# Sliding-window attention and a GELU layer on one core: key loads on a second queue, chunked V copies, other engines for three evictions

## The chip, the core and the metric

The kernel runs on one core of a Trainium2 chip. The core has TensorE (matrix products, into the accumulator memory PSUM), VectorE, ScalarE and GpSimd (elementwise work), SyncE (which issues transfers here) and 16 DMA engines. In the profile they are PE (and PEld for its weight loads), DVE, ACT, POOL and SP. The metric is the device time of one execution in microseconds.[...]

## What is computed

Attention over 8 batches of 8 heads, 576 positions and 64 features, in which a position sees only those up to 32 away; its result, as 4608 tokens of 512 features, goes through a layer with 2048 hidden features and a tanh-GELU.

```python
scores = scale * np.matmul(q, k.transpose(0, 1, 3, 2))
mask = np.abs(pos[:, None] - pos[None, :]) <= window          # window = 32
scores = np.where(mask, scores, -1000000000.0)
attn = softmax(scores)                                        # cut: row maximum, exp, sum
attn_out = np.matmul(attn, v)
x = attn_out.transpose(0, 2, 1, 3).reshape(B * S, H * D)      # 4608 x 512
h = x @ w_in                                                  # 512 x 2048
g = 0.5 * h * (1.0 + np.tanh(c * (h + 0.044715 * h * h * h)))
out = g @ w_out                                               # 2048 x 512
```

## The kernel before

The tokens are split into 9 tiles of 512. Tile t goes through `ffn_in` (512-wide products with w_in, then GELU on ScalarE) and `ffn_out` (products with w_out). Beside the `ffn_out` of tile t the attention of batch t+1 is computed, piece by piece: a plan says ahead of which matmul of `ffn_out` (its place, `i`) which piece is put into the program. In the plans, s is the scores of a pair of heads, m their mask, v their sums and values with the inversion of the sums on ScalarE, x the product that writes them to the tokens, and d the copy of one chunk of V. The number after the letter is the pair of heads (−1: the last positions of the batch before), the number after @ a PSUM buffer.

```python
PLAN = {4: "s0@0 s1@1 v-1", 16: "m0 m1 x-1", 33: "s2@0 v0@1 v1", 36: "m2", ...}     # tiles 2 to 6
PLAN_1 = {12: "s0@0 s1@1 s2", 16: "m0 m1", 36: "m2", 45: "v0@1 v1 s-1@0", 52: "x0", 55: "x1", 62: "m-1",
          69: "s3@0 v2 v-1@1", 73: "m3", 81: "x2", 85: "x-1", 91: "v3 s4@1", 112: "x3 m4"}   # tile 1
PAIR_1 = {17: slice(0, 4), 40: slice(4, 8)}
```

Queries and keys are loaded as fp32, cast to fp16 on VectorE and transposed by DMA. For batch 2 the loads are put into the program near the end of tile 0, and the V loads stand behind the key transposes on SyncE.

```python
def load_qk(b):
    ...
    nc.sync.dma_start(qr, q[b, :, 0:512, :].rearrange("h (p j) d -> p h (j d)", j=4))
    for c in range(4):
        nc.sync.dma_start(kr[:, c, :, :],
                          k[b, :, 128 * c:128 * c + 128, :].rearrange("h p d -> p h d"))
    nc.sync.dma_start(qt, ...)          # the last 64 positions
    nc.sync.dma_start(kt, ...)

def keys():                             # in tile 1, behind the casts of the queries, two combines and sums
    for pr in range(NPAIR):
        nc.vector.tensor_copy(k16[:, pr, :, :, :], kr[:, :, 2 * pr:2 * pr + 2, :])
        if pr % 2:
            nc.sync.dma_start_transpose(KTs[b % 2][...], k16[...])
    if b == 2:
        for c in range(4):
            nc.sync.dma_start(vr[:, c, :, :], v[b, ...])
```

The values need V twice: as loaded, and with the two halves of its 128 partitions shifted against each other (slots 4 to 7). For batch 2 GpSimd casts the four chunks, and `pair_v` copies the shifted half on VectorE, four heads at a time; `pair_chunk`, which tile 0 uses, copies one chunk of all heads.

```python
def pair_v(b, copy, hs=slice(0, H)):
    copy(V[64:128, 4:8, hs, :], V[64:128, 0:4, hs, :])
    copy(V[0:64, 4:7, hs, :], V[0:64, 1:4, hs, :])

def pair_chunk(b, c, copy):
    copy(V[64:128, 4 + c, :, :], V[64:128, c, :, :])
    if c:
        copy(V[0:64, 3 + c, :, :], V[0:64, c, :, :])
...
            if t == 1 and i in PAIR_1:
                pair_v(2, nc.vector.tensor_copy, PAIR_1[i])
```

Tile 0 has four accumulators of 128 tokens, finished in the order 0, 3, 1, 2. Accumulator 0 is in the bank that the first `ffn_in` of tile 1 takes. The other tiles use a product scheme with fewer matmuls (seven products of 16 matmuls each, n = 0 to 6), whose two banks take turns: product 0 and then 2 in one, product 1 and then 3 in the other, and product 4 takes the first one again. So the bank has to be read between product 0 and 2 (`M1`), and between 2 and 4 (`C11`).

```python
# ffn_out_0, tile 0
(nc.scalar.copy if t4 > 1 else nc.vector.tensor_copy)(yo, pys[t4])
# ffn_out, tiles 1 to 8
if n == 0:
    nc.vector.tensor_copy(M1, py)                                    # L653
elif n == 1:
    nc.vector.tensor_tensor(U2, py, M1, op=ALU.add)                  # L655
elif n == 2:
    (nc.vector.tensor_copy if t > 1 else nc.scalar.copy)(C11, py)    # L657
```

Of the kernel before, what the change touches and what calls it, by code (L numbers as in the profile page):

```python
# [36 lines left out]
def cut(b):  # L37
# [5 lines left out]

PLAN = {4: "s0@0 s1@1 v-1", 16: "m0 m1 x-1", 33: "s2@0 v0@1 v1", 36: "m2", 44: "x0", 50: "x1",
        62: "s3@0 s4@1 v2", 66: "m3", 80: "x2", 84: "m4", 91: "v3", 112: "x3"}


# [4 lines left out]
          29: "w2", 33: "s-1@1 n0@0", 35: "e0", 36: "m2", 37: "k3", 38: "w5", 39: "m-1", 40: "r3@1", 43: "e1",  # L54
          46: "s3@0 v-1@1 d0", 47: "w3 e2", 48: "d1 m3", 51: "n2@0", 52: "e3 d2 d3 x-1",
          55: "u3 p0@0 p2@1 x0 x1", 56: "e4 x2 x3", 60: "c1"}
PLAN_1 = {12: "s0@0 s1@1 s2", 16: "m0 m1", 36: "m2", 45: "v0@1 v1 s-1@0", 52: "x0", 55: "x1", 62: "m-1",
          69: "s3@0 v2 v-1@1", 73: "m3", 81: "x2", 85: "x-1", 91: "v3 s4@1", 112: "x3 m4"}
PAIR_1 = {17: slice(0, 4), 40: slice(4, 8)}

ORDER_0 = [(t4, 4 * w + i) for w in range(3) for i in ((0, 2, 3, 1), (0, 2, 1, 3), range(4))[w] for t4 in (0, 1, 3, 2)] + \
          [(t4, 12 + i + j) for i in (0, 2) for t4 in (0, 3, 1, 2) for j in range(2)]
# [7 lines left out]
def kernel(  # L70
# [9 lines left out]
    nc = tc.nc  # L80
# [82 lines left out]
    def load_qk(b):  # L163


        qr = rawp.tile([128, H, 256], FP32, name="qr")
        kr = rawp.tile([128, 4, H, 64], FP32, name="kr")
        qt = tailp.tile([16, H, 256], FP32, name="qt", tag="vt")
        kt = tailp.tile([64, H, 64], FP32, name="kt", tag="tr")
        raws[b] = (qr, kr, qt, kt)  # L170
        nc.sync.dma_start(qr, q[b, :, 0:512, :].rearrange("h (p j) d -> p h (j d)", j=4))
        for c in range(4):
            nc.sync.dma_start(kr[:, c, :, :],  # L173
                              k[b, :, 128 * c:128 * c + 128, :].rearrange("h p d -> p h d"))
        nc.sync.dma_start(qt, q[b, :, 512:576, :].rearrange("h (p j) d -> p h (j d)", j=4))  # L175
        nc.sync.dma_start(kt, k[b, :, 512:576, :].rearrange("h p d -> p h d"))

# [9 lines left out]
    def pair_v(b, copy, hs=slice(0, H)):  # L187

        V = Vs[b % 2]
        copy(V[64:128, 4:8, hs, :], V[64:128, 0:4, hs, :])  # L190
        copy(V[0:64, 4:7, hs, :], V[0:64, 1:4, hs, :])  # L191
# [143 lines left out]
    def bank(i):  # L335

        return psM.tile([128, 512], FP32, name="mm", tag=f"x{i}")
# [140 lines left out]
    def weigh(b, g, pair=None):  # L478
        pe = groups.pop((b, g))
        if pair is not None:  # L480
            od = psS.tile([128, 2, 512], FP32, name="ps_od", tag=f"S{pair}")
            o, d = od[:, 0, :], od[:, 1, :]
        else:
            o = psO.tile([128, 512], FP32, name="ps_o", tag="O")
            d = psO.tile([128, 512], FP32, name="ps_d", tag="D")
        sum_up(b, g, d, pe)
        times(b, g, o, pe)
        return o, d
# [101 lines left out]
    pys = {}  # L590

    def store(t, t4, yo, cols=slice(0, 512), *engs):

        m = i = 0
        while m < 128:
            b, c = divmod(t * 512 + t4 * 128 + m, S)
            q0, n = (0, cut(b)) if c < 4 * cut(b) else (cut(b), 144 - cut(b))
            j, p = divmod(c - 4 * q0, n)
            e = min(n - p, 128 - m)
            nj = 1 if p else max(1, min(4 - j, (128 - m) // n))  # L600
            eng = engs[i % len(engs)] if engs else nc.gpsimd
            if nj > 1:
                e = nj * n
                eng.dma_start(out_v[b, j:j + nj, q0:q0 + n, cols], yo[m:m + e, cols])
            else:
                eng.dma_start(out_v[b, j, q0 + p:q0 + p + e, cols], yo[m:m + e, cols])  # L606
            m += e
            i += 1
# [3 lines left out]
    def ffn_out_0(t4, fc):  # L612
        new = t4 not in pys
        if new:
            pys[t4] = bank(t4) if t4 < 2 else psO.tile([128, 512], FP32, name="py3", tag="OD"[t4 % 2])
        nc.tensor.matmul(pys[t4], gTs[0][:, fc, t4 * 128:t4 * 128 + 128], w_out16[:, fc, :],
                         start=new, stop=(fc == NF - 1))
        if fc == NF - 1:
            if "yo" not in pys:
                pys["yo"] = hp.tile([128, 2, 512], FP32, name="yo2", tag="qt16")  # L620
            yo = pys["yo"][:, t4, :] if t4 < 2 else yp.tile([128, 512], FP32, name="yo", tag="yo")
            (nc.scalar.copy if t4 > 1 else nc.vector.tensor_copy)(yo, pys[t4])  # L622
            later.append((t4, yo))

    def ffn_out(t, i):

        n, blk, f = i // 16, i // 8 % 2, i % 8
        a, w, new = WINO[n]
        end = t == NT - 1
        if i % 16 == 0 and new:  # L630
            pys[n % 2] = bank((1 + n) % 2)
            if end and n == 4:
                pys["apart"] = psO.tile([128, 512], FP32, name="py2", tag="O")
        py = pys[n % 2].rearrange("p (b c) -> p b c", b=2)
        apart = end and blk and n in (4, 6)
        if a[0] == "A":
            r0, c0 = 8 * (int(a[2]) - 1) + f, 256 * (int(a[1]) - 1) + 128 * blk
            lhsT = gTs[t][:, r0, c0:c0 + 128]
        else:
            lhsT = wino[a][:, f, 128 * blk:128 * blk + 128]  # L640
        one = end and n in (4, 6)
        nc.tensor.matmul(pys["apart"][:, 0:256] if apart else py[:, blk, :], lhsT,  # L642
                         wino[w][:, f, :], start=(new and i % (8 if one else 16) == 0),
                         stop=(i % (8 if one else 16) == (7 if one else 15)),
                         skip_group_check=True)
        if i % 16 < 15:
            return
        yo, left, right = wino["yo"], slice(0, 256), slice(256, 512)
        C11, C12, C21, C22 = (yo[:, r:r + 2, c] for r in (0, 2) for c in (left, right))

        M1, U2, U3 = C21, C12, C22
        if n == 0:
            nc.vector.tensor_copy(M1, py)  # L653
        elif n == 1:
            nc.vector.tensor_tensor(U2, py, M1, op=ALU.add)  # L655
        elif n == 2:
            (nc.vector.tensor_copy if t > 1 else nc.scalar.copy)(C11, py)  # L657
            if end:
                for x in range(2):
                    store(t, x, yo[:, x, :], left, nc.sync)  # L660
        elif n == 3:
            nc.vector.tensor_tensor(U3, py, M1, op=ALU.add)
        elif n == 4:
            if not end:
                nc.vector.tensor_tensor(C22, py, U3, op=ALU.add)
            else:
                for x, part in enumerate((py[:, 0, :], pys["apart"][:, 0:256])):
                    nc.vector.tensor_tensor(C22[:, x, :], part, U3[:, x, :], op=ALU.add)
                    store(t, 2 + x, yo[:, 2 + x, :], right, nc.sync, nc.scalar)
        elif n == 5:  # L670
            nc.vector.tensor_tensor(C21, py, M1, op=ALU.add)  # L671
            for x in range(2):
                store(t, 2 + x, yo[:, 2 + x, :], *((left, nc.sync, nc.scalar) if end else ()))
# [78 lines left out]
    s0 = psS.tile([128, 2, 512], FP32, name="ps_o", tag="S0")  # L752
# [63 lines left out]
    for t in range(NT):  # L816
        b = t + 1
        att = b < B
        if t:
# [6 lines left out]
            for fc in range(begun, NF):  # L826
# [12 lines left out]
                if t > 1 and fc == 8 and att:  # L839
                    pair_v(b, nc.vector.tensor_copy)  # L840
        plan = PLAN_0 if not t else PLAN_1 if t == 1 else PLAN if att else {5: "v-1", 31: "x-1"} if t == B - 1 else {}

# [5 lines left out]
        if t and b + 1 < B:  # L848
            load_qk(b + 1)
        ods = {}  # L850
        for i in range(113 if t else 65):
# [3 lines left out]
            for act in plan.get(i, "").split():  # L855
# [49 lines left out]
                elif kind == "v":  # L905
                    bb, gg = group(g)
                    o, d = weigh(bb, gg, at)
# [7 lines left out]
            if t == 1 and i == 30:  # L915
                cast_vt(2)
                store(0, *later[0])
                store(0, *later[2])
            if t == 1 and i in PAIR_1:
                pair_v(2, nc.vector.tensor_copy, PAIR_1[i])  # L920
            if t == 0 and i < 64:
                ffn_out_0(*ORDER_0[i])
            elif t and i < 112:
                ffn_out(t, i)
# [36 lines left out]
```

## Time and profile before

| what | value |
|---|---|
| median of 3 runs | 301.06 us (300.74 to 307.55) |
| span of the profiled execution | 299.5 us |
| instructions | 7127 |
| moved by DMA | 50.73 MB, 169 GB/s on average |
| granted TensorE clock | 0.998 |

The profile's times are in us from the start of the span. A line of the timeline has the start, the time, the engine, the line of the program, the operation and what it writes from what it reads; a count at its end (x4) means that several were merged. Square brackets give how long the engine stood idle ahead of it, and what it was waiting for. A line of the windows has the stretch, its length, the busy time of PE, PEld, DVE, ACT and POOL with their counts, the granted clock, the mean share of the time in which a DMA engine was busy (over 1 where transfers overlap in an engine) and GB/s. SPq is the queue in which SyncE issues transfers: the time of such a line is that of the issue, not of the transfer.

### The profile page before, as it was taken

What the parts mean: (1) busy time and instruction counts of PE and PEld (TensorE: products, weight loads), DVE (VectorE), ACT (ScalarE), POOL (GpSimd) and SP (SyncE); (2) the same over time, 40 slices, a digit from 0 to 9 for tenths busy, and PEclk for the clock granted to TensorE, in tenths of its full rate; (3) what the DMA queues carried; (4) which work ended last, traced back from release to release, by engine and by line L of the source; (5) the groups of instructions that cost most, each with busy time, mean ns of one, the idle gap of its engine ahead of it and who ended that gap; (6) DMA issues with size and microseconds to landing.
All of it is one profiled execution on the core that took longest, in us unless ns stands there. A gap on an engine that the chain in (4) does not pass through costs nothing.

```text
span 299.5 us, 7127 instructions
## 1 busy us (share of the span) xinstructions
PE 287.0 (96%) x2893; PEld 179.6 (60%) x2893; DVE 194.4 (65%) x438; ACT 194.1 (65%) x308; POOL 91.0 (30%) x141
## 2 busy tenths in 40 slices
PE   7889999999899999999999999999999999999994
PEld 3534444446674488448854885478547864784583
DVE  4753577898865975867696769766876635442452
ACT  5866767779586786578566956695678666606600
POOL 3435425202656060605080606060700050016000
PEclk9999999999999999999999999999999999999999
DMA  7999999899799979998999996989694031004013
GB/s 221 266 306 382 354 286 239 230 191 205 188 213 216 244 201 178 168 136 211 176 181 151 220 171 154 146 212 174 106 167 51 3 103 39 2 4 138 2 35 105
DMA packets 116519, 50.73 MB, mean 169 GB/s; under 512 B 98008, under 2 KB 110040, under 8 KB 116487
## 3 DMA queue, kind: packets, MB, share of 16 engines
q1 hardware_dynamic: 87428, 37.88, 62.0%
q0 software_dynamic: 27936, 11.35, 25.2%
q10 hardware_dynamic: 1122, 1.06, 1.1%
q8 instruction: 22, 0.36, 0.5%
q14 instruction: 11, 0.08, 0.1%
HBM read 36.70 MB, written 9.44 MB: 154 GB/s over the span
## 4 chain that ended last, share of the span: by engine, by line
PE 64%; DMA 21%; SPq 7%; ACT 4%; DVE 2%; issue 1%; POOL 0%
PE mm L642 28%; PE mm L544 15%; PE ph L544 13%; DMA KT<-k 5%; DMA tr<-in_q_dram 4%; DMA wst<-in_moe_w_in_dram 3%; DMA wst<-in_moe_w_out_dram 3%; SPq L173 3%; DMA kt<-in_k_dram 3%; PE ps_s L435 2%; DMA vr<-in_v_dram 2%; PE ps_d L462 2%; DMA tr<-in_k_dram 2%; SPq L227 2%; PE ps_o L472 2%; SPq L175 1%
## 5 line engine op out<-in xcount | busy, mean ns | idle before, releaser
L544 PEld LDWEIGHTS <-w_in 128*128 128x128 f16 x576 | 56.1, 98 | 66.6 <-issue 0.9
L544 PE MATMUL mm<-xT,w_in 128*128 128x512 f16 x304 | 74.7, 379 | 0.4 <-DVE yo L622 0.4
L552 ACT ACTIVATE gT<-mm 128x512 f16<-128x512 f32 x76 | 45.1, 597 | 39.9 <-PE mm L544 39.2
L544 PE MATMUL ph<-xT,w_in 128*128 128x512 f16 x272 | 68.2, 379 | 0.4 <-POOL w_in L758 0.4
L606 POOL DMA_DIRECT2D out_dram<-y x55 | 32.7, 604 | 87.4 <-DVE y L671 74.4
L642 PEld LDWEIGHTS <-s 128*128 128x128 f16 x512 | 49.6, 98 | 6.8 <-issue 0.8
L587 DVE TENSOR_TENSOR s<-gT 128x512 f16<-128x512 f16 x64 | 27.2, 426 | 32.1 <-ACT gT L552 32.1
L552 ACT ACTIVATE gT<-ph 128x512 f16<-128x512 f32 x68 | 37.9, 600 | 13.3 <-PE ph L544 13.3
L642 PE MATMUL mm<-t,s 128*128 128x256 f16 x376 | 44.9, 273 | 0.7 <-ACT y L657 0.7
L642 PEld LDWEIGHTS <-gT 128*128 128x128 f16 x384 | 36.0, 98 | 6.6
L448 ACT ACTIVATE pe<-ps_s 128x960 f16<-128x960 f32 (+1 forms) x31 | 29.5, 975 | 13.6 <-PE ps_s L435 13.5
L642 PE MATMUL mm<-w_out,gT 128*128 128x256 f16 x256 | 32.8, 273 | 0.0
L95 ACT ACT_TABLE_LOAD x18 | 23.1, 1283 | 2.2 <-issue 1.9
L498 ACT ACTIVATE lt<-lt 128x480 f32<-128x480 f32 (+3 forms) x36 | 21.1, 585 | 1.1
L497 ACT ACTIVATE lt<-ps_d 128x480 f32<-128x480 f32 (+2 forms) x28 | 15.6, 556 | 9.4 <-PE ps_d L462 6.3
L457 DVE TENSOR_TENSOR pe<-pe,band 128x960 f16<-128x960 f16 x28 | 18.3, 668 | 2.7 <-ACT pe L448 2.7
L181 POOL DMA_DIRECT2D V<-in_v_dram x20 | 17.9, 913 | 0.8 <-issue 0.4
L472 PEld LDWEIGHTS <-V 128*64 128x64 f16 x520 | 13.9, 111 | 7.1 <-DVE V L191 2.4
L642 PE MATMUL mm<-t,gT 128*128 128x256 f16 x128 | 16.3, 273 | 0.0
L435 PE MATMUL ps_s<-QT,KT 64*64 64x128 f16 (+3 forms) x576 | 13.5, 216 | 1.3 <-DMA KT<-k 0.5
L853 POOL COPY after<-KL 128x1 f16<-128x1 f16 x5 | 1.7, 339 | 42.5 <-DMA KL<-kt 42.5
L435 PEld LDWEIGHTS <-KT 64*64 64x64 f16 x576 | 10.0, 106 | 7.5 <-issue 3.4
(111 smaller groups left out, 336.7 us busy)
## 6 DMA issues: line engine op xcount, KB each, us to landing
kr<-in_k_dram SPq DMA_DIRECT2D x31, 256.0 KB, 11.4
qr<-in_q_dram SPq DMA_DIRECT2D x6, 1024.0 KB, 8.1
wst<-in_moe_w_in_dram SPq DMA_DIRECT2D x7, 512.0 KB, 8.2
V<-in_v_dram POOLq DMA_DIRECT2D x20, 128.0 KB, 8.5
wst<-in_moe_w_out_dram SPq DMA_DIRECT2D x2, 1024.0 KB, 11.9
wst<-in_moe_w_out_dram SPq DMA_DIRECT2D x4, 512.0 KB
qr<-in_q_dram SPq DMA_DIRECT2D x7, 256.0 KB, 6.8
out_dram<-y POOLq DMA_DIRECT2D x6, 192.0 KB, 5.9
```

The source lines that it names most:

```text
L95: nc.scalar.add_instruction(mybir.InstLoadActFuncSet(name=nc.get_next_instruction_name(), act_func_set_id=which, ins=[], outs=[]))
L181: nc.gpsimd.dma_start(V[:, c, :, :], v[b, :, 128 * c:128 * c + 128, :].rearrange("h p d -> p h d"))
L435: nc.tensor.matmul(sides[h][64 * half:64 * half + 64, 4 * n * r:4 * n * r + 4 * n].rearrange("k (j p) -> k j p", j=4)[:, :, p0 - q0:p1 - q ...
L448: nc.scalar.activation(pe, ps[:, :, 0:w], AF.Exp, scale=SCALE)
L457: nc.vector.tensor_tensor(pe, pe, m.rearrange("k (o j) p -> k o j p", o=1).broadcast_to(list(pe.shape)), op=ALU.mult)
L472: nc.tensor.matmul(o[64 * h:64 * h + 64, cols].rearrange("d (j p) -> d j p", j=4)[:, :, p0 - q0:p1 - q0], Vs[b % 2][:, slot, 2 * pr + h, : ...
L498: nc.scalar.activation(lt[:, 0:n], lt[:, 0:n], AF.Exp, scale=-1.0)
L544: nc.tensor.matmul(ph, w_in16[:, dc, fc * 128:fc * 128 + 128], xT[:, dc, t * 512 % RING:t * 512 % RING + 512], start=(dc == 0), stop=(dc = ...
L552: nc.scalar.activation(gTs[t][:, fc, :], phs[fc], AF.Gelu_apprx_tanh)
L587: nc.vector.tensor_tensor(dst, x, y, op=op)
L606: eng.dma_start(out_v[b, j, q0 + p:q0 + p + e, cols], yo[m:m + e, cols])
L642: nc.tensor.matmul(pys["apart"][:, 0:256] if apart else py[:, blk, :], lhsT, wino[w][:, f, :], start=(new and i % (8 if one else 16) == 0) ...
```

## The change

It has five parts. The chunks 2 and 3 of batch 2's keys are issued by ScalarE instead of SyncE. The shifted copy of batch 2's V is made chunk by chunk, at the places 14, 20 and 24, so that the first chunks needn't wait for the last; with it, most pieces of tile 1's plan move some places forward. Of tile 0's accumulators, number 0 goes to ScalarE and number 2 to VectorE. The bank `C11` of tile 1 goes from ScalarE to VectorE, as in the other tiles. In tiles 2 to 6 the first scores stand at place 7 instead of 4, so that the transposed keys have more time to land.

```diff
-PLAN = {4: "s0@0 s1@1 v-1", 16: "m0 m1 x-1", 33: "s2@0 v0@1 v1", 36: "m2", 44: "x0", 50: "x1",
+PLAN = {7: "s0@0 s1@1 v-1", 16: "m0 m1 x-1", 33: "s2@0 v0@1 v1", 36: "m2", 44: "x0", 50: "x1",
         62: "s3@0 s4@1 v2", 66: "m3", 80: "x2", 84: "m4", 91: "v3", 112: "x3"}
 ...
-PLAN_1 = {12: "s0@0 s1@1 s2", 16: "m0 m1", 36: "m2", 45: "v0@1 v1 s-1@0", 52: "x0", 55: "x1", 62: "m-1",
-          69: "s3@0 v2 v-1@1", 73: "m3", 81: "x2", 85: "x-1", 91: "v3 s4@1", 112: "x3 m4"}
-PAIR_1 = {17: slice(0, 4), 40: slice(4, 8)}
+PLAN_1 = {12: "s0@0 s1@1 s2", 14: "d0 d1", 16: "m0 m1", 20: "d2", 24: "d3", 36: "m2", 40: "v0@1 v1 s-1@0", 46: "x0", 50: "x1",
+          60: "m-1", 65: "s3@0 v2 v-1@1", 71: "m3", 82: "x2", 85: "x-1", 88: "v3 s4@1", 112: "x3 m4"}
 ...
         for c in range(4):
-            nc.sync.dma_start(kr[:, c, :, :],
-                              k[b, :, 128 * c:128 * c + 128, :].rearrange("h p d -> p h d"))
+            (nc.scalar if b == 2 and c > 1 else nc.sync).dma_start(
+                kr[:, c, :, :], k[b, :, 128 * c:128 * c + 128, :].rearrange("h p d -> p h d"))
 ...
-            (nc.scalar.copy if t4 > 1 else nc.vector.tensor_copy)(yo, pys[t4])
+            (nc.scalar.copy if t4 in (0, 3) else nc.vector.tensor_copy)(yo, pys[t4])
 ...
         elif n == 2:
-            (nc.vector.tensor_copy if t > 1 else nc.scalar.copy)(C11, py)
+            nc.vector.tensor_copy(C11, py)
 ...
-            if t == 1 and i in PAIR_1:
-                pair_v(2, nc.vector.tensor_copy, PAIR_1[i])
```

## The prediction

> **What bounds the kernel now.** I began with the busy times of the whole span.
>
> ```profile
> PE 287.0 (96%) x2893; PEld 179.6 (60%) x2893; DVE 194.4 (65%) x438; ACT 194.1 (65%) x308; POOL 91.0 (30%) x141
> ```
>
> TensorE sits idle for 299.5 − 287.0 = 12.5 us, and most of that is at the start and the end, which the change leaves alone. So the most that the change can win is the idle time of TensorE between tile 0's end (about 56 us) and tile 7. To see where that lies I asked for busy time by tile, one window for each of tiles 1 to 4, cut where the first `mm L544` of a tile starts.
>
> ```profile
> 56.50:89.23 32.73, 31.29 (x350) 20.47 (x350) 26.02 (x55) 25.84 (x43) 9.73 (x15) 1.00 1.07 198
> 89.23:120.09 30.86, 30.65 (x333) 20.16 (x331) 22.20 (x50) 21.84 (x34) 11.23 (x17) 1.00 1.28 208
> 120.09:150.90 30.81, 30.48 (x331) 20.05 (x330) 22.22 (x49) 21.54 (x33) 9.49 (x15) 1.00 1.22 172
> 150.90:181.38 30.48, 30.48 (x331) 20.04 (x330) 22.33 (x53) 21.54 (x33) 11.22 (x17) 1.00 1.14 175
> ```
>
> The first two numbers of a line are its length and TensorE's busy time. Tile 1 loses 1.44 us, tile 2 0.21, tile 3 0.33, tile 4 nothing. The timeline of TensorE names the gaps in brackets; these five lines are all of them from 56 us on that exceed its reporting threshold.
>
> ```profile
> 56.49 0.81 PE L544 MATMUL mm<-xT,w_in 128*128 128x512 f16 x3 [0.41 <-DVE yo L622]
> 77.58 0.38 PE L472 MATMUL ps_od<-pe,V 128*64 128x64 f16 x12 [0.74 <-DVE V L191]
> 81.52 0.70 PE L642 MATMUL mm<-t,s 128*128 128x256 f16 x5 [0.66 <-ACT y L657]
> ...
> 103.85 0.62 PE L435 MATMUL ps_s<-QT,KT 64*64 64x96 f16 x32 [0.21 <-DMA KT<-k]
> ...
> 134.66 0.62 PE L435 MATMUL ps_s<-QT,KT 64*64 64x96 f16 x32 [0.33 <-DMA KT<-k]
> ```
>
> Sum: 0.41 + 0.74 + 0.66 + 0.21 + 0.33 = 2.35 us, 0.8% of the time. Each part of the change is aimed at one of them. **No faster result than about 298.7 us is in reach**, whatever else happens.
>
> [...]a copy of V with 512 elements on 64 partitions takes 0.29 us, one with 1024 takes 0.42, so half of the work costs 0.69 of the time.
>
> **Part 1, tile 0's accumulators.** Tile 1's first matmul needs the bank of row block 0, whose last matmul ends at 54.8 us, but VectorE reaches that copy only at 55.76 because four products `xT L507` (2.35 us from 53.49) stand before it; it ends at 56.45. ScalarE at that time has done a cast (53.62 to 54.24) and is idle for 1.02 us. With the change it first issues two key loads, then copies block 0. A key load of that size took 0.57 us to issue on SyncE[...] (start 77.33), so two end at 54.24 + 1.2 = 55.4; the copy (0.59) ends at about 56.05, and TensorE, free at 56.08, goes straight on: **−0.4 us**. Block 3 follows on ScalarE at 56.6; the table load (1.28) ends at 57.9, still ahead of the first gelu (58.4). VectorE has blocks 1 and 2 after its combine, by 58.2, as late as before. Its bank is next needed 12 x 0.22 us and more after the start of tile 1, so nothing waits.
>
> **Part 2, two key loads on ScalarE.** Here are SyncE's queue and, for two of the microseconds in it, the DMA engines (the last two columns: share busy, GB/s).
>
> ```profile
> 50.84 0.62 SPq L171 DMA_DIRECT2D qr<-in_q_dram  x1
> 51.50 9.10 SPq L173 DMA_DIRECT2D kr<-in_k_dram  x4
> 60.70 0.76 SPq L175 DMA_DIRECT2D qt<-in_q_dram  x1
> ```
>
> ```profile
> 59.00:60.00 1.00, 1.00 (x7) 0.45 (x5) 1.00 (x3) 1.00 (x3) 0.00 (x0) 1.00 0.28 55
> 60.00:61.00 1.00, 1.00 (x6) 0.43 (x5) 1.00 (x3) 0.91 (x2) 0.00 (x0) 1.00 0.50 115
> ```
>
> Four issues need 9.1 us[...]; the third alone runs from 55.9 to 59.7. While SyncE stands in it, the DMA engines run dry: (1 − 0.28) + (1 − 0.50) = 1.2 us of them are lost.[...] So all of the batch's bytes can be down some 1.2 us sooner. Against it stands the query load: it landed at 58.95[...]. From the rates above I estimate 0.8 to 2 us of delay for it. VectorE casts queries first, then does two combines and one set of sums, then casts the keys at 64.85, for which it had waited 0.69. So the keys are cast between 0.1 us later and, at a delay of 2 us, 1.3 later, or 0.7 sooner without any delay. I call δ the gain at V's loads (now issued from 68.39 on); I put it at 0.3 us, between −1 and +1.
>
> **Part 3, V chunk by chunk, and the new places in tile 1.** Now VectorE waits for the fourth cast, as these lines of POOL and of VectorE show.
>
> ```profile
> 75.30 1.34 POOL L302 CAST V<-qr 128x512 f16<-128x512 f32 x2 [1.24 <-DMA qr<-in_v_dram]
> ```
>
> ```profile
> 73.52 0.68 DVE L653 COPY y<-mm 128x512 f32<-128x512 f32 x1
> 74.11 1.31 DVE L457 TENSOR_TENSOR pe<-pe,band 128x960 f16<-128x960 f16 x2
> 76.67 0.42 DVE L190 COPY V<-V 64x1024 f16<-64x1024 f16 x1 [1.24 <-POOL V L302]
> ```
>
> The casts end at 72.98, 74.06, 75.97 and 76.64. Copying is not cheaper: 7 x 0.29 = 2.0 us against 0.42 + 0.42 + 0.42 + 0.78 = 2.0. What changes is the order. Chunks 0 and 1 now stand ahead of the eviction L653: chunk 1 waits for its cast, ends at 74.06 + 0.58 = 74.65 − δ, L653 at 75.25 − δ. TensorE wants that bank at place 32, 74.45 after part 1: **a new wait of up to 0.8 − δ**. The masks end at 76.45 − δ, chunk 2 at 77.0 − δ, chunk 3 at 77.6 − δ. Values v0, now at place 40 instead of 45, need all four: TensorE is there at 75.25 − δ + 8 x 0.109 = 76.1 − δ and stands for up to 1.4 us. It leaves v0 at 77.75 − δ, as before, but with five places (0.55 us) still to do. So the gap moves and grows; what was won in part 1 is given back here.
>
> **Part 4, tile 1's bank on VectorE.** Now ScalarE copies C11 behind two inversions and an exponential, ends at 81.47, and TensorE stands 0.66. VectorE has it after x0: with v0 at 77.75 − δ, Ln and Exp 1.2, x0 0.65, copy 0.61, it is done at 80.3 − δ. TensorE needs it at place 64, at 79.2 − δ + 16 x 0.109 = 80.95 − δ: no wait. Against the present 81.52 that is **−0.57 − δ**, and this is the whole balance of parts 1, 3 and 4 at this point: about −0.9 us with δ = 0.3. The rest of the tile has the same work.
>
> **Part 5, scores at place 7.** In tiles 2 and 3 TensorE waits at place 4 for transposed keys. Those land at a time that SyncE and the DMA engines set: for tile 2 the chain of waits runs from the key loads at 77.33 through `DMA kt` (7.67 us) and `DMA KT<-k` to 103.85. If they land when they do now, three places of 0.109 done ahead of them win 0.33 us, no more, however much earlier TensorE arrives. If V is down sooner by δ, so are these, about. So through tile 2 the win is 0.33 + δ = 0.6 us, less than the 0.9 + 0.2 that TensorE could use. In tile 3 the casts start with the tile itself, so its 0.33 comes on top. ScalarE isn't held: it loads its table until 105.15, later than scores at place 7 end. Later tiles have no gap to lose. **Sum: 0.6 + 0.33, about −0.95 us**, 301.06 − 0.95 = 300.1.
>
> **Rivals.** (a) The gain in full: the query load isn't slowed, δ reaches 1 and the keys of batch 3 move up with it. For it speaks the 1.2 us of idle DMA. Then nearly all of 2.35 us is saved: 298.8. (b) The order on VectorE becomes the limit: δ is −1, chunk 1 holds up L653 and both masks, v0 stands longer, and the keys of batch 3 are 1 us late. For it speaks that VectorE is busy 26.0 of tile 1's 32.7 us and has no slack between 73.5 and 82. It makes 301.4 or so. (c) ScalarE's issues are held up like SyncE's (up to 4.0 us each). Then block 0 is copied late, and tile 1 starts 1 to 3 us late: 302 to 304. Against it: [...]its two loads at the start of the kernel took 0.50 and 0.49 us.
>
> **Range and chances.** My middle path gives 300.1 us. The floor is the 298.7 of the first section; upward (b) seems as likely as (a), and (c) less. 298.8 to 301.6 should hold 8 times in 10. Two per cent are 6.0 us: faster by that is out of reach, slower needs (c) at its worst in two places: chances 0.01, 0.97 and 0.02.
>
> **What would show it.** Part 1: no wait of `mm L544` near 56 us, and two ScalarE issues of about 0.6 us each near 54.5. Part 2: a DMA share over 0.8 from 59 to 61 us; query casts that start after 59.0. Part 3: TensorE waiting for `V L195` or `L197` at v0, and perhaps on `y L653` near 74.5. Part 4: no wait on L657 in tile 1. Part 5: no wait for `KT<-k` in tile 3, and a shorter or no wait in tile 2. The prediction falls if ScalarE's issues take over 1 us, if the keys of tile 2 land much earlier or later than 103.5, or if tiles 4 to 7 change length.

## The result and the profile after

The changed kernel takes 302.62 us (median; 302.56 to 302.67) against 301.06 before. The ratio, from four executions of it and two of the kernel before (301.06 and 300.74), is 1.0057, with a 95% interval of 1.0033 to 1.0081. In a repetition beside many more executions of the kernel before it is 1.0033 (1.0010 to 1.0057), about 1.0 us. So it is slower, by less than 2%, and the forecast range of 298.8 to 301.6 missed it. Disturbed executions are left out of all ratios here; the profiles of e3, f2, g4 and i2 come from such ones, in which tile 2 stands 4.5 to 6.1 us for its keys, so of these only tile 1 is read.

First the busy times of the whole span in the changed kernel, then its tiles 1 to 3 (length, TensorE's busy time, and so on), cut as before.

```profile
PE 287.1 (95%) x2893; PEld 179.6 (60%) x2893; DVE 196.6 (65%) x442; ACT 193.7 (64%) x307; POOL 92.1 (31%) x141
```

```profile
57.52:91.28 33.76, 31.60 (x352) 20.63 (x350) 27.45 (x60) 25.45 (x41) 11.53 (x16) 1.00 1.17 195
91.28:121.73 30.45, 30.45 (x332) 20.02 (x330) 22.39 (x50) 21.48 (x33) 11.07 (x16) 1.00 1.25 197
121.73:152.15 30.42, 30.42 (x333) 20.03 (x330) 22.25 (x49) 21.55 (x34) 9.40 (x15) 1.00 1.24 180
```

TensorE does the same work, but tile 1 is 1.02 us longer (33.76 against 32.74), and tiles 2 and 3 are 0.24 and 0.40 us shorter (before: 30.69, from 89.23 to 119.92, and 30.82, to 150.74; the prediction's cuts behind these tiles stand some 0.17 us late). Tile 1 also begins 1.03 us later, at 57.52. The gaps of TensorE from tile 0's end to tile 3, in the timeline of the changed kernel:

```profile
55.80 0.59 PE L615 MATMUL mm<-w_out,gT 128*128 128x512 f16 x2 [0.79 <-POOL w_out L214]
76.46 1.03 PE L641 MATMUL mm<-w_out,gT 128*128 128x256 f16 x8 [0.38 <-DVE y L652]
79.07 0.25 PE L471 MATMUL ps_od<-pe,V 128*64 128x64 f16 x4 [1.16 <-DVE V L196]
79.69 0.25 PE L471 MATMUL ps_od<-pe,V 128*64 128x64 f16 x4 [0.37 <-DVE V L196]
87.89 0.42 PE L471 MATMUL ps_o<-pe,V 128*64 128x96 f16 x14 [0.21 <-DVE xT L506]
```

The waits on `yo`, on `C11` and on `KT` are all gone. In tile 1 there are 2.12 us of waits instead of 1.40: for product 0's bank, for V, and 0.21 for `xT`, ahead of the values v3. The first line is a wait for w_out in tile 0, behind a load that the change doesn't touch. Why V is late is in the timelines of GpSimd and VectorE of the changed kernel:

```profile
76.23 1.78 POOL L301 CAST V<-qr 128x512 f16<-128x512 f32 x1 [1.85 <-DMA qr<-in_v_dram]
```

```profile
75.73 0.68 DVE L652 COPY y<-mm 128x512 f32<-128x512 f32 x1
76.33 1.21 DVE L456 TENSOR_TENSOR pe<-pe,band 128x960 f16<-128x960 f16 x2
78.05 0.67 DVE L194 COPY V<-V 64x512 f16<-64x512 f16 x1 [0.51 <-POOL V L301]
```

The third cast takes 1.78 us; in the kernel before it took 0.61 (the two of the prediction's line, 1.34 us, have 0.11 between them). It runs while VectorE multiplies the two masks, which the chunk copies have pushed back from 17.6 to 18.8 us after the start of tile 1, and it ends 0.47 us after them.

### The profile page after: what moved, and what is told of

Read it like the earlier page. It is cut to its first block, busy times and chain, and to the rows that moved or that the text cites. A ratio compares the mean times of both kernels' runs of the same rounds, so it can differ in the third digit from the quotient of the medians.

```text
span 300.8 us, 7128 instructions
## 1 busy us (share of the span) xinstructions
PE 287.1 (95%) x2893; PEld 179.6 (60%) x2893; DVE 196.6 (65%) x442; ACT 193.7 (64%) x307; POOL 92.1 (31%) x141
## 4 chain that ended last, share of the span: by engine, by line
PE 71%; DMA 19%; SPq 4%; DVE 2%; POOL 1%; issue 0%; ACT 0%; DVEq 0%
PE mm L641 31%; PE mm L543 18%; PE ph L543 14%; DMA wst<-in_moe_w_in_dram 5%; DMA tr<-in_q_dram 4%; DMA kr<-in_k_dram 4%; DMA wst<-in_moe_w_out_dram 3%; PE ps_s L434 3%; PE ps_d L461 2%; DMA qr<-in_v_dram 2%; DMA tr<-in_k_dram 2%; PE ps_o L471 2%; SPq L226 2%; SPq L136 1%; SPq L172 1%; POOL V L301 1%
## 5 line engine op out<-in xcount | busy, mean ns | idle before, releaser
L497 ACT ACTIVATE lt<-lt 128x480 f32<-128x480 f32 (+3 forms) x36 | 21.1, 586 | 1.1
L641 PE MATMUL mm<-w_out,s 128*128 128x256 f16 x120 | 14.4, 273 | 0.0
L586 DVE TENSOR_TENSOR s<-s,gT 128x512 f16<-128x512 f16 x32 | 13.6, 425 | 1.1
L506 DVE TENSOR_TENSOR xT<-ps_o,lt 128x480 f16<-128x480 f32 (+5 forms) x26 | 13.4, 536 | 1.1 <-PE ps_o L471 1.1
```

Source lines behind the costliest of these rows:

```text
L497: nc.scalar.activation(lt[:, 0:n], lt[:, 0:n], AF.Exp, scale=-1.0)
L586: nc.vector.tensor_tensor(dst, x, y, op=op)
```

## The experiments

Three theories at first. **V**: the order on VectorE and the early places cost the time. **K**: the key loads on ScalarE do. **H**: it is the start of the kernel, which differs from execution to execution. The numbers behind each verdict are in the table at the end of this section.

**e1_before_again** is the kernel before, unchanged.

> The kernel before, unchanged, for a second trace and a measure of how much the part ahead of tile 1 moves by itself. In the first traces tile 1 starts 1.2 us later in the changed kernel (57.7 against 56.5 us), though nothing ahead of 54 us is changed. Theory H (head): that is mere variation of the loads at the start, so here the start of tile 1 should lie anywhere from 56 to 58 us, and the ratio 1.000 within 0.004. Theories V and K (below): the ratio is 1.000 and the start of tile 1 within 0.3 us of 56.5.

Ratio 1.000 (0.9977 to 1.0022). Tile 1 starts at 57.38 instead of 56.49, and the wait for w_out in tile 0 (0.78 us) is there too. So H is right about the 1.03 us in the start and that gap: neither needs the change. (The first trace of the change starts tile 1 at 57.52, not at the 57.7 of the expectation.) But it doesn't explain a ratio that is repeated.

**e2_chunks_only**: the kernel before with the chunks and the new places of tile 1.

```diff
-PLAN_1 = {... 16: "m0 m1", 36: "m2", 45: "v0@1 v1 s-1@0", ...};  PAIR_1 = {17: ..., 40: ...}
+PLAN_1 = {... 14: "d0 d1", 16: "m0 m1", 20: "d2", 24: "d3", 36: "m2", 40: "v0@1 v1 s-1@0", ...}
```

> The kernel before with the chunked V copy and the new places in tile 1 alone. Theory V (order on VectorE and values too early): this part alone costs time, +0.5 to +1.2 us, with waits of TensorE for the bank of product 0 (some 0.4 us) and for the V copies (1 us and more) and still a wait on ScalarE's C11. Theory K (key loads on ScalarE are what costs): within 0.3 us of before, since V lands as in the kernel before. Theory H: as before within its noise.

1.0018 (0.9995 to 1.0040), not told from before by its time; tile 1 takes 33.86 us, with waits of 0.20 for product 0's bank and of 1.16 + 0.37 for V. V's waits are there without any load on ScalarE, and C11's, which theory V still expected, is hidden behind them. The third cast takes 1.62 us. The trace favours V, not K.

**e3_no_chunks**: the changed kernel with V's halves and the old places.

```diff
-PLAN_1 of the change
+PLAN_1 and PAIR_1 of before
```

> The changed kernel with the V copy by halves and the places of tile 1 as they were before. Theory V: the four other parts win, 0.8 to 1.5 us less than before (0.4 at tile 0's end, about 0.6 at C11, 0.3 to 0.5 in tiles 2 and 3). Theory K: no better than before, V's casts still end at 77 us or later. Theory H: whatever the start of tile 1 does.

0.9968 (0.9942 to 0.9993): about 1 us below before, as V said. Against the changed kernel (1.0033 in its repetition) this difference is clear: chunks and early places, added to the other parts, are the loss.

**e4_no_act_loads**: the changed kernel with all key loads on SyncE.

```diff
-(nc.scalar if b == 2 and c > 1 else nc.sync).dma_start(kr[:, c, :, :], ...)
+nc.sync.dma_start(kr[:, c, :, :], ...)
```

> The changed kernel with all key loads on SyncE again. Theory V: no better than the changed kernel, 0 to 0.5 us slower, with the waits of TensorE at product 0's bank and at the V copies as large as there. Theory K: 0.5 to 1.2 us faster than the changed kernel, with V's casts done about 1 us sooner after the start of tile 1 and the query casts not held up. Theory H: as the changed kernel, within the variation of the start.

1.0007 (0.9985 to 1.0028). That is 0.8 us below the changed kernel's repetition, as K forecast, but the intervals overlap; the trace is as V said. The waits at product 0's bank (0.35) and at V (1.16 + 0.37) are as large as with the loads on ScalarE, V's casts end as long after the start of tile 1 (21.0 us; 21.1 in the changed kernel), and the third cast takes 1.52 us. g3 and g4 below go on with K. Its tile 1 took 35.27 us (55.61 to 90.88), 1.59 more than f1's; what made it so long wasn't settled, so its end isn't read.

The traces then gave a sharper theory, **M**: the masks hold up GpSimd's cast. Its rivals: **D**, V's bytes land later, and **P**, the earlier places cost by themselves.

**f1_after_again** is the changed kernel, unchanged.

> The changed kernel unchanged, beside many runs of the kernel before on this chip, and a second trace. In the first pair of traces tile 1 is 1.02 us longer and tiles 2 and 3 are 0.66 us shorter together, while the part ahead of tile 1 differs by 1.0 us though its instructions are the same but for the end. Theory M (the masks are moved onto GpSimd's cast of V's third chunk and hold it up): a ratio of 1.000 to 1.002, the rest of the first 1.7 us having been the start; the third cast takes 1.5 us or more again. Theory D (V's bytes themselves land later with the change): the ratio stays near 1.005 and V's third chunk lands over 1 us later after its issue than in the kernel before.

1.0033 (1.0010 to 1.0057). Tile 1 is 33.68 us, the third cast takes 1.40. V's third chunk is cast 24.14 us after SyncE's first key load (23.92 in the first trace; 23.80 and 22.33 in the two of before). M's cast is there; its ratio is above what M said. The fourth chunk separates M from D. In f1 and in the first trace of the change it landed 24.87 and 24.70 us after the first key load, in the two of before 24.40 and 24.46: 0.47 and 0.24 us are D's. The casts then ended 1.23 and 1.56 us behind this landing instead of 0.67 and 0.68: 0.56 and 0.88 us are M's. That the later landing comes from the change isn't shown: it lies between 24.02 and 25.32 in the nine traces with chunk copies, and between 23.78 and 25.01 in the ten without.

**f2_masks_first**: the changed kernel, masks ahead of the chunks.

```diff
-14: "d0 d1", 16: "m0 m1", 20: "d2", ...
+16: "m0 m1 d0 d1", 20: "d2", ...
```

> The changed kernel with the two masks and product 0's bank ahead of the first two chunk copies on VectorE. Theory M: the masks end before V's third chunk is there, its cast takes 0.6 to 0.7 us instead of 1.5 to 1.8, the wait for product 0's bank (0.38) is gone, v0's waits (1.16 and 0.37) shrink to about 0.7 in sum, tile 1 is 0.8 to 1.2 us shorter than in the changed kernel. Theory D: V lands as late, the cast ends as late, tile 1 is shorter by the 0.38 us at most.

1.0001 (0.9974 to 1.0027), an interval that overlaps f1's. On VectorE and on GpSimd:

```profile
74.39 1.37 DVE L456 TENSOR_TENSOR pe<-pe,band 128x960 f16<-128x960 f16 x2
```

```profile
75.64 0.62 POOL L301 CAST V<-qr 128x512 f16<-128x512 f32 x1 [1.31 <-DMA qr<-in_v_dram]
```

The masks are through at 75.76, and the cast takes 0.62 us. The wait for product 0's bank is gone. But V's waits sum to 1.41, and tile 1 is only 0.4 us shorter than in f1 (33.30): half of what M promised. The chunk copies now stand where the masks stood, and the way from V's last cast to the end of the tile is 13.02 us.

**f3_places_as_before**: the changed kernel, the other pieces at their old places.

```diff
-40: "v0@1 v1 s-1@0", 46: "x0", 50: "x1", 60: "m-1", 65: "s3@0 v2 v-1@1", ...
+45: "v0@1 v1 s-1@0", 52: "x0", 55: "x1", 62: "m-1", 69: "s3@0 v2 v-1@1", ...
```

> The changed kernel, V's chunks where the change has them, but all other pieces of tile 1 at the places of the kernel before (v0 at 45 and so on). Theory M: the held-up cast stays (1.5 us or more), v0's wait is shorter by five places (0.55 us) but the work behind it less by as much: tile 1 as long as in the changed kernel within 0.3 us. A third theory, P (the earlier places themselves cost): tile 1 is 0.5 to 1 us shorter than in the changed kernel.

1.0013 (0.9986 to 1.0040). P is right: tile 1 is 32.71 us, 0.97 below f1, although the third cast is as slow as ever (1.80). (What I wrote for M was a slip: if v0 leaves at the same time with five places more behind it, tile 1 is shorter by these.) And what tile 1 won was lost again in tile 2, in its lengths of f3:

```profile
89.37:121.15 31.78, 30.49 (x333) 20.06 (x331) 22.14 (x50) 21.78 (x34) 10.91 (x16) 1.00 1.34 202
```

1.29 us of it are a wait for `KT`.

**f4_masks_twice**: the kernel before, each mask multiplied twice (it is 0 or 1).

```diff
-16: "m0 m1", 36: "m2", ...
+16: "m0 m1 m0 m1", 36: "m2", ...
```

> The kernel before with each of the masks of groups 0 and 1 in tile 1 multiplied twice (the mask is 0 or 1, so the values stay). The second pair falls into time in which VectorE waited 1.24 us for V's casts. Theory M: it runs beside the casts of V's third and fourth chunk, which take 1.2 us longer in sum; the V copies start about 1.2 us later, and v0's wait grows from 0.74 to 1.5 to 2 us. Theory D: VectorE only fills its idle time; the casts take 0.61 to 0.73 us each, and v0's wait stays below 0.9 us.

1.0040 (1.0018 to 1.0061), and v0's wait grows to 1.31 us. But this time the third chunk had come early and only the fourth cast met the masks, and VectorE's V copies start at 78.00 right behind the fourth mask: the delay is VectorE's own. So neither the wait nor the time tells M from D. What does is this pair, on GpSimd and on VectorE:

```profile
75.96 0.95 POOL L302 CAST V<-qr 128x512 f16<-128x512 f32 x1 [1.53 <-DMA qr<-in_v_dram]
```

```profile
75.79 0.65 DVE L457 TENSOR_TENSOR pe<-pe,band 128x960 f16<-128x960 f16 x1
```

```profile
76.36 1.06 DVE L457 TENSOR_TENSOR pe<-pe,band 128x960 f16<-128x960 f16 x1
```

The cast came in between the second mask and the third: it took 0.95 us instead of 0.61 and ended 0.47 us after the second mask, and the third mask took 1.06 instead of 0.64. Each holds up the other.

Next, where a gain in tile 1 goes. **O**: the order in tile 1 is the whole loss. **T**: tile 2, waiting for its keys, takes back what tile 1 wins. **A**: the loads on ScalarE cost by themselves.

**g1_evictions_and_place7**: the kernel before with only the three evictions and place 7.

> The kernel before with only the three evictions on other engines and the scores of tiles 2 to 6 at place 7. Theory O (the order and the places of V in tile 1 are the loss, and these parts win): 0.5 to 1.2 us less than before; no wait on C11, v0's wait at place 45 up to 0.4 longer. Theory T (what tile 1 wins, tile 2 loses in waiting for its keys): tile 1 is 0.3 to 0.7 us shorter, but tile 2 stands 0.5 us or more at its scores, and the time is within 0.3 us of before.

0.9991 (0.9967 to 1.0016). Tiles 1 and 2 of it, and its one gap in tile 2:

```profile
56.87:88.55 31.68, 31.27 (x351) 20.71 (x350) 27.25 (x58) 25.15 (x41) 9.44 (x15) 1.00 1.11 199
88.55:120.05 31.50, 30.48 (x332) 20.05 (x330) 22.20 (x50) 21.77 (x34) 10.41 (x16) 1.00 1.29 202
```

```profile
104.31 0.62 PE L435 MATMUL ps_s<-QT,KT 64*64 64x96 f16 x32 [1.02 <-DMA KT<-k]
```

Tile 1 wins 1.06 us against the first trace, tile 2 loses 0.81. The trace is as T said; the ratio's interval still reaches into O's forecast.

**g2_masks_first_old_places**: the changed kernel with f2's order and f3's places. **g4_g2_without_act_loads**: the same, with all key loads on SyncE.

```diff
-14: "d0 d1", 16: "m0 m1", 20: "d2", 24: "d3", 36: "m2", 40: "v0@1 v1 s-1@0", ...
+16: "m0 m1 d0 d1", 20: "d2", 24: "d3", 36: "m2", 45: "v0@1 v1 s-1@0", ...
```

> The changed kernel with V's chunk copies behind the masks and all other pieces of tile 1 at their places of before. Theory O: both losses are undone, tile 1 takes about 32.3 us (33.7 in the changed kernel), and the time is 0.5 to 1.2 us below the kernel before. Theory T: tile 1 as said, but tile 2 gives at least half of it back in a wait for KT. A third theory, A (the key loads on ScalarE cost by themselves): no better than before, 0.3 us or more above the run without these loads.

> The run before the last one, with all key loads on SyncE: masks first, old places, the evictions and place 7. Theories O and T: as the run with these loads, within 0.3 us. Theory A: 0.3 us or more below it, and the best of all.

0.9982 (0.9961 to 1.0003) and 0.9993 (0.9969 to 1.0017). g2's tile 1 is 33.21 us, not the 32.3 that O expected; the chunk copies stand beside the casts, of which the third and fourth took 1.77 us from start to end (1.34 in the kernel before), and v0 waits three times, 1.65 us together. A got no support: taking the loads off ScalarE didn't help.

**g3_act_loads_only**: the kernel before with the two loads on ScalarE.

> The kernel before with the two key loads on ScalarE and nothing else. Theories O and T: within 0.3 us of before, the key casts start as long after SyncE's first key load as before (13.1 to 13.4 us). Theory A: 0.5 us or more above before.

0.9997 (0.9969 to 1.0024). The keys are cast 13.65 us after the first key load, in the two traces of before 13.35 and 12.80. Theory A, with 0.5 us or more, isn't borne out (the interval ends at 0.7 us); this part does nothing that can be seen.

**h2_early_places_only**: the kernel before with the change's places of tile 1, V in halves.

> The kernel before with only the places of tile 1 from the change (values v0 at 40 instead of 45, and so on); V is still copied in halves, with all else as before. Theory P (values ahead of V's arrival): v0's wait grows by about 0.55 us, to 1.0 to 1.4, the wait on C11 stays, tile 1 is 33.0 to 33.4 us, and the time is 0.3 to 0.7 us above before. Theory M (the loss is the chunks' order on VectorE): tile 1 is 32.4 to 32.8 us as before.

1.0010 (0.9987 to 1.0032), not told from before by its time. Tile 1 started at 57.87 and took 32.39 us; from V's last cast to its end it took 12.92 us, 0.33 more than the kernel before. Its length is what M forecast; P's 33.0 to 33.4 missed. C11's wait all but vanishes behind that for V (product 4 starts 0.28 us late), which P had not seen: with V in halves the early places cost 0.33 us, with chunks 0.87 (f1 against f3).

**h3_later_scores_only** and **h1_evictions_later_scores**: the scores of tiles 2 to 6 at place 14, in the kernel before and in g1.

```diff
-PLAN = {7: "s0@0 s1@1 v-1", 16: "m0 m1 x-1", 33: "s2@0 v0@1 v1", 36: "m2", 44: "x0", 50: "x1", ...
+PLAN = {14: "s0@0 s1@1 v-1", 24: "m0 m1 x-1", 41: "s2@0 v0@1 v1", 44: "m2", 52: "x0", 57: "x1", ...
```

> The kernel before with only the scores of tiles 2 to 6 at place 14 (and the pieces behind them later). Theory T: the waits for KT in tiles 2 and 3 (0.54 us together in the first trace, 0.63 in the second) are gone and nothing else changes: 0.4 to 0.8 us below before. Rival W: tiles 4 to 6, which had no wait, are longer than 30.48 us.

> The three evictions on other engines as in the change, and the scores of tiles 2 to 6 at place 14 with the pieces behind them moved by 2 to 8 places. Theory T (tile 2's keys take back what tile 1 wins): no wait for KT in tiles 2 and 3, tile 1 at 31.7 to 32.4 us and tiles 2 and 3 at 30.4 each, 1.0 to 1.8 us below the kernel before. Rival W (the pieces pushed to later places wait for each other on ScalarE and VectorE): tiles 2 to 6 are each 0.3 us or more longer, and the time is no better than before.

0.9989 (0.9972 to 1.0007) and 0.9979 (0.9951 to 1.0006), neither told from before. In h3 tiles 2 to 6 take 30.4 us each, without a wait; W is out. In h1 tile 2 stood 2.04 us even so: the keys came 17.5 us after its start, 14.6 in the first trace. (The trace of h1 is a long one, 303.49 us where the median is 301.08; its tile 2 took 34.13 us, with a stretch in which 16 products took 3.21 us; 16 at the end of the same tile took 1.91.)

**i1_both_limits_lifted**: g2 with the scores at place 14. **i2_evictions_scores_at_10**: g1 with the scores at place 10 and the pieces behind them 1 to 4 places later.

> The changed kernel with the chunk copies behind the masks, tile 1's other pieces at their old places, and the scores of tiles 2 to 6 at place 14. If the two limits are the whole story: tile 1 ends 11.7 to 12.2 us after V's last cast (12.59 in the kernel before), tiles 2 and 3 take 30.4 us each, 0.6 to 1.2 us below the kernel before. If not: a new wait appears, or the time is within 0.3 us of before.

> The three evictions on other engines, all V and key loads as before, and the scores of tiles 2 to 6 at place 10. If the two limits are the whole story: tile 1 ends 11.9 us after V's last cast, tiles 2 and 3 take 30.4 us unless the keys land later than 15 us after tile 1's end, 0.6 to 1.2 us below before. If not: within 0.3 us of before.

i1: 0.9973 (0.9946 to 1.0000); tile 1 ends 12.66 us after V's last cast, not the 11.7 to 12.2 forecast, since v0 waits 1.24 us for the chunk copies; and tile 2 still waits 0.85 us for keys. So the two limits aren't the whole story. i2: 0.9937 (0.9902 to 0.9972), more than was forecast; tile 1 ends 11.90 us after V's last cast. It and e3 are the only versions whose interval lies below 1. Both have the evictions and none of the chunk copies.

The table has the traces that carry the argument. "Fourth chunk" is when the last chunk of V landed, "to the casts' end" the end of its cast, both from SyncE's first key load of batch 2 on; "to the end" goes from there to tile 2's first matmul (us).

| trace | tile 1 starts | third cast | fourth chunk | to the casts' end | to the end | tile 1 |
|---|---|---|---|---|---|---|
| before | 56.49 | 0.61 | 24.46 | 25.14 | 12.59 | 32.74 |
| e1 (before) | 57.38 | 0.62 | 24.40 | 25.07 | 12.59 | 32.37 |
| h3 (before, later scores) | 56.85 | 0.90 | 24.11 | 24.86 | 12.59 | 32.00 |
| g3 (before, loads on ScalarE) | 56.72 | 0.61 | 24.76 | 25.43 | 12.60 | 33.04 |
| g1 (evictions) | 56.87 | 0.61 | 24.17 | 24.84 | 11.90 | 31.68 |
| f3 (change, old places) | 56.66 | 1.80 | 24.03 | 25.65 | 11.83 | 32.71 |
| after | 57.52 | 1.78 | 24.70 | 26.26 | 12.71 | 33.76 |
| f1 (after) | 56.92 | 1.40 | 24.87 | 26.10 | 12.70 | 33.68 |

## Why the prediction was wrong

**Part 1** removed its wait, and ScalarE's two issues took 1.01 us together (1.2 forecast). No run has it alone, but the table leaves it no gain: the four traces with the old evictions and places end tile 1 12.59 or 12.60 us after V's last cast, whether it starts 4.99 us after the first key load (before) or 5.45 (h3). An earlier start only makes v0 wait longer (0.74 us before, none over 0.2 in h3). The prediction saw the gain given back in part 3; the runs show that V's casts are the clock of the tile in all of them.

**Part 2** is where δ fails. The DMA engines are kept busy, as forecast; here are the same two microseconds in the changed kernel:

```profile
59.00:60.00 1.00, 1.00 (x6) 0.49 (x5) 0.69 (x2) 0.12 (x1) 0.00 (x0) 1.00 1.36 221
60.00:61.00 1.00, 1.00 (x7) 0.41 (x5) 1.00 (x4) 1.00 (x3) 0.00 (x0) 1.00 1.37 218
```

Yet the keys are cast 13.10 us after SyncE's first load instead of 13.35, and the queries 7.37 instead of 7.49: the delay of 0.8 to 2 us that I estimated for the queries isn't there, and neither is a gain. V's third chunk came 0.1 us later than before. So δ, put at 0.3, is about zero or below (V's fourth chunk landed 0.24 us later), and alone (g3) the part changes nothing. That ScalarE's issues would bring the batch's bytes down 1.2 us sooner was my estimate from the idle DMA share; g3's ratio of 0.9997 shows nothing of it.

**Part 3** is the step that failed. Its order was right: the new wait for product 0's bank (0.8 − δ forecast, 0.38 measured), and v0's wait (up to 1.4 forecast, 1.53). That the second figure fits is partly luck: the casts ended later than forecast, and tile 1 also began later, 5.21 us after the first key load instead of 4.58. The step took the casts' times from the kernel before and set the masks beside them as if they were free. They aren't: with the masks over it, the third cast took 1.40 to 1.80 us in after, f1, f3, e2 and e4, and in after, f1 and f3 it ended 0.47 or 0.48 us after the second mask; it took 0.61 to 0.62 in f2, g1 and e1, where they are out of its way. From the fourth chunk's landing to the casts' end this made 1.56 and 1.23 us (after, f1) instead of 0.68 and 0.67. f4 shows the hold-up in both directions: the cast took 0.95 us instead of 0.61, and the mask behind it 1.06 instead of 0.64. Why the two engines hold each other up, no trace shows.

The sign of it stood in the trace of the kernel before, on GpSimd and on VectorE:

```profile
72.08 0.90 POOL L302 CAST V<-qr 128x512 f16<-128x512 f32 x1 [16.34 <-DVE s L587]
73.25 0.81 POOL L302 CAST V<-qr 128x512 f16<-128x512 f32 x1 [0.27 <-DVE s L587]
```

```profile
72.08 0.42 DVE L587 TENSOR_TENSOR s<-s,gT 128x512 f16<-128x512 f16 x1
72.43 0.83 DVE L587 TENSOR_TENSOR s<-gT 128x512 f16<-128x512 f16 x1
73.18 0.41 DVE L587 TENSOR_TENSOR s<-gT,s 128x512 f16<-128x512 f16 x1
```

The first two casts took 0.90 and 0.81 us where the other two took 0.61. They lie over VectorE's sums, and end 0.48 and 0.47 us after one of these; the sum between them took 0.83 us instead of 0.42.

**Part 4** removed the wait on C11, and with the old places that is worth 0.7 us (12.59 to 11.90 in g1, 11.83 in f3). But its sum has a slip. Part 3 says that five places (0.55 us) are still to do behind v0; part 4 leaves them out. From v0 (77.75) to place 48 (79.2) it has 1.45 us; the kernel before takes 1.37 there (77.58 to 78.95) with three places instead of eight. With all eight, TensorE comes to place 64 at about 81.4 − δ, and the gain is 0.1 + δ, not 0.57 + δ. Measured from V's last cast to place 64 it is 0.21: 4.67 us (78.57 to 83.24) instead of 4.88. Behind place 64 the tile takes 0.33 us longer (8.04 instead of 7.71, of which 0.21 are the wait at v3), where the prediction said that the rest has the same work; h2, with the early places alone, has the same 0.33.

So at place 64, counted from the first key load, the forecast was −0.87 us and the first pair of traces has +0.91. The 1.78 us between them are 0.54 of δ (0.24 later instead of 0.3 sooner), 0.88 of hold-up on the third cast, and 0.36 of the slip. In the second pair (e1, f1: +0.80) they are 0.77, 0.56 and 0.34.

**Part 5**: tiles 2 and 3 went from 61.51 to 60.87 us, 0.64 less, without a wait (in the second pair, e1 and f1, 0.24 less; f1's tile 3 still waits 0.39). Tile 2's share says little, since tile 1 ended late and gave the keys time. The limit by tile 2's keys was right: where tile 1 ended sooner, tile 2 stood 1.02 us (g1) and 1.29 (f3).

The sum from the first key load on: 1.12 (casts) + 0.12 (way to the end) − 0.64 (tiles 2 and 3) = +0.60 us in the first pair, 1.03 + 0.11 − 0.24 = +0.90 in the second, near the 1.0 us of the repeated ratio. The forecast was −0.95. Of the rest of the first 1.56 us, 0.81 is the start of the kernel: the first key load of batch 2 was issued at 52.31 us instead of 51.50, with the same program ahead of it. Nor was 301.06 a firm base: in the later comparisons the kernel before had medians from 301.63 to 302.22. The range left no room for that. Of the rivals, (b) named the right engine, with VectorE's order as the limit and a time of 301.4; (a) and (c) didn't come.

How the loss divides between the hold-up and the early places is read from traces; by time no run tells them apart. Open is also how e3, g1, h1 and i2 compare: their intervals overlap, i2 rests on nine executions without a trace of tile 2 that can be read, and why the keys come 14.6 us after the start of tile 2 in one trace and 17.5 in another was not settled.

## What to carry to other kernels

Before an instruction is moved into a gap of one engine, see what its neighbour does there: here two VectorE masks of 128x960, laid over a GpSimd cast of 128x512, made the cast two to three times as long (1.40 to 1.80 us instead of 0.61), and the trace shows it as a longer instruction, not as a wait. Casts of one shape that take 0.61 and 0.90 us in the same trace are the sign to look for. Where a stage's end keeps the same distance from the arrival of one operand in several traces, whatever its start (12.59 or 12.60 us in four of them here), work moved ahead of that arrival wins nothing, and a consumer put earlier only waits longer. And a gain in one stage is real only if the next can use it: of the 1.06 us that the evictions won in tile 1 of g1, tile 2 gave back 0.81 in waiting for its keys.

## What was not expected of the hardware

A GpSimd cast of 128x512 (0.61 us) and a VectorE mask of 128x960 (0.64 us) that overlap cost 0.3 to 0.4 us each in f4, and up to 1.2 us for the cast where two masks came in a row (1.80 us in f3). Held-up casts end 0.47 or 0.48 us after the mask or sum that they lay over, in five traces (before, after, f1, f3 and f4). The same program starts tile 1 at 56.5 us or at 57.4 (before and e1), with a wait of 0.78 us for w_out in the second; why isn't known.
